# Column sums of squares on TensorE: a bfloat16 product of ones with the upper halves of the words in place of a float32 product

## The chip, the cores and the metric

The kernel runs on one core of one Trainium2 chip. The metric is the device time of one launch in microseconds (us), the median of several runs. Each of the core's engines works through a list of instructions of its own, in order: TensorE (PE: matrix products; its weight loads are shown apart, as PEld), VectorE (DVE), ScalarE (ACT), GpSimd (POOL) and SyncE (SP, which issues the DMAs here). They wait for each other on semaphores.

## The reference, cut to what matters

Two branches work on the same input x (2048 tokens, width 576) and a gate mixes them, token by token:

```python
g = sigmoid((x * gate_w).sum(-1, keepdims=True))
a = attention(x, wq, wk, wv, wo, beta)   # 32 heads of 18, 4 segments of 512 tokens, memory over segments
b = (gelu(x @ w_gate) * (x @ w_up)) @ w_down   # inner width 4608
return g * a + (1 - g) * b
```

Everything is float32. The kernel computes each product in pairs of float16 words: a number is scaled by a power of two, its float16 rounding is the upper word, the rest is the lower word, and a product takes three matrix products (high by high, high by low, low by high). The powers of two come from sums of squares of the operands, and this is all that these sums are for: a scale is read from the exponent of such a sum.

## The kernel before

**Stages.** The program first loads x and the attention weights and finds their scales (to about 25 us). Then the projections of the four segments run (to about 215 us). Then 72 steps follow, 36 tiles of the inner width by 2 halves of the tokens; `step(v)` interleaves the feed-forward products of a tile with the attention of the heads (lines 1263 `down`, 532 `product`, 1383 nested products, 1178 `scores`, 1216 `values`). Two tiles make a block of four steps, and a block takes 72.5 us. From about 1480 us the last down products and the output projection run (line 1739).

**Order of the work.** PE, ACT, DVE and POOL execute their instructions in the order in which the code issues them; nothing is moved by a planner. What makes an engine wait is data, a PSUM bank or a buffer that isn't free yet.

**A scale.** `sum_squares` (DVE) or `act_square` (ACT, line 89) squares a tile and leaves a sum for each partition in one column of a small tile: `wst` for the attention weights and the first x, `stat` for the feed-forward weights. The sum over the partitions is a matrix product with a 128x128 tile of ones: `sums` (line 94), with 10, 5 or 3 columns. DVE adds up the columns of the result (lines 108, 187 or 268) and makes the powers of two from the exponent.

**Where `sums` stands.** It is called 24 times:

- in the first 25 us four times, from `scale_x(0)`, `scale_sum(4)`, `scale_v` and `scale_sum(0)`, on `wst`;
- 19 times on `stat`, from `scales`: once in the projections of the last segment (159 us), once in the first step (215 us), then once in a block, in its second step, up to 1442 us;
- once from `scale_sum(2)`, in the last step (1472 us), on `wst`, for the output weights.

The tile of ones is float32 (`ones`), and so are `wst` and `stat`. Such a product stands as one instruction in the program's list and as two weight loads and two passes in the trace. A second tile of ones, `onesb`, is bfloat16; it is used for the 30 warm-up products at the start (line 819) and for the sums of squares of x (line 176).

Of the kernel before, what the change touches and what calls it, by code (L numbers as in the profile page):

```python
# [8 lines left out]
F32 = mybir.dt.float32  # L9
BF16 = mybir.dt.bfloat16  # L10
# [8 lines left out]
P = 128  # L19
# [24 lines left out]
def kernel(ctx: ExitStack, tc: tile.TileContext, xs, wqk, wv, wo, wgu, wd, beta, out):  # L44
    nc = tc.nc
    pe, act, dve, pool, sp = nc.tensor, nc.scalar, nc.vector, nc.gpsimd, nc.sync

    cst = ctx.enter_context(tc.tile_pool(name="cst", bufs=1))
# [4 lines left out]
    def bank(tag, bufs=1, dt=F32):  # L53
        return ps.tile([P, 512 if dt == F32 else 1024], dt, name=tag, tag=tag, bufs=bufs)
# [4 lines left out]
    def spare():  # L59

        turns["n"] += 1
        if not turns["of"]:
            return bank("st", 2)
        return bank("V") if turns["n"] % 3 == 0 and turns["of"] == 3 else bank("dn", 2)
# [26 lines left out]
    def sums(st, o=None):  # L91

        o = (spare() if o is None else o)[:, : st.shape[1]]
        pe.matmul(o, ones, st, start=True, stop=True)
        return o

    def scale_of(i, total):
# [8 lines left out]
    def scale_sum(i, st, o=None):  # L106
        t = wts.tile([P, 1], F32, name="sv", tag="sv", bufs=2)
        dve.tensor_reduce(t, sums(st, o), AX.X, OP.add)
        scale_of(i, t)
# [69 lines left out]
    def scale_x(c):  # L179
        one = slice(c, c + 1)  # L180
        n = x2[:, one]
        if c:
            norm_x(c, bank("pv") if c == 1 else spare())
            dve.tensor_scalar(n, n, x2[:, c - 1 : c] if c % 2 else 1e-30, None, OP.max)
        else:
            n = wts.tile([P, 1], F32, name="sv", tag="sv", bufs=2)
            dve.tensor_reduce(n, sums(wst[:, 5:10]), AX.X, OP.add)
            dve.tensor_scalar(n, n, 1e-30, None, OP.max)
        v = cst.tile([P, 2], F32, name="xv", tag="xv", bufs=2)
        root(v[:, 0:1], v[:, 1:2], n)  # L190

        dve.tensor_scalar(xsc[:, one], v[:, 1:2], 2.0**-52, None, OP.mult)
        dve.tensor_scalar(xis[:, one], v[:, 0:1], 2.0**51, None, OP.mult)
        x16[c] = wts.tile([P, 9, L], F16, name="x16", tag="x16", bufs=4)
# [69 lines left out]
    def scales(fb, o=None):  # L264

        o = sums(stat[fb % 2].rearrange("p a b -> p (a b)"), o)
        z = wts.tile([P, 6], F32, name="z", tag="z", bufs=2)
        dve.tensor_reduce(z[:, 4:6], o.rearrange("p (a b) -> p a b", a=2), AX.X, OP.add)
        dve.tensor_scalar(z[:, 0:4], x2, z[:, 4:5], 1e-30, OP.mult, OP.max)
        v = wts.tile([P, 2, 2], F32, name="v", tag="v", bufs=2)  # L270
        pb = wts.tile([P, 2, 4], F32, name="pb", tag="pb", bufs=3)
        dve.tensor_scalar(v[:, 0].bitcast(I32), z[:, 4:6].bitcast(I32), 1, EXP, OP.logical_shift_right, OP.bitwise_and)
        dve.tensor_scalar(pb[:, 0].bitcast(I32), z[:, 0:4].bitcast(I32), EXP, None, OP.bitwise_and)
        dve.tensor_scalar(v[:, 1].bitcast(I32), v[:, 0].bitcast(I32), EXP, None, OP.bitwise_xor)
        dve.tensor_scalar(pb[:, 1].bitcast(I32), pb[:, 0].bitcast(I32), EXP, None, OP.bitwise_xor)
        scl_a[fb] = v, pb
# [220 lines left out]
        oms.append(dram.tile([HT, D], F32, name="om"))  # L497
        oas.append(dram.tile([HT, 9 * P], F16, name="oa"))

    ones = cst.tile([P, P], F32, name="ones")  # L500
    onesb = cst.tile([P, P], BF16, name="onesb")
    mask = cst.tile([P, L], BF16, name="mask")
    gate = cst.tile([P, 3, 16], F32, name="gate")
# [51 lines left out]
    with tc.tile_pool(name="prj", bufs=2, side="right", reuse_waits="tile") as pp:  # L555
# [256 lines left out]
        FIRST = (0,)  # L812
        with tc.manual_schedule(engines=ORDERED):
            pool.memset(onesb, 1.0)
            pool.memset(ones, 1.0)

            start = bank("G")
            for _ in range(30):
# [293 lines left out]
    with tc.tile_pool(name="keep", bufs=2, side="right", reuse_waits="tile") as kp, ExitStack() as tail:  # L1112
# [679 lines left out]
        with tc.manual_schedule(engines=ORDERED):  # L1792
# [21 lines left out]
            for t in range(16):  # L1814
                for n in range(2):
                    down(fb, t, n)
                if t in (1, 2):
                    f, c, o, g = ends.pop(0)
# [80 lines left out]
```

## Time and profile before

| | us |
|---|---|
| median of 3 runs | 1559.5 |
| lowest and highest run | 1559.41, 1560.13 |
| span of the profiled execution, first to last instruction | 1558.8 |
| PE busy | 1552.4 |
| PE weight loads busy | 953.9 |
| DVE busy | 1264.4 |
| ACT busy | 1205.9 |
| POOL busy | 1133.1 |

The page gives no time for the profiled execution beside its span; the median of the runs stands 0.7 us above it. Busy times of matmuls overlap, since a matmul starts while the one before it still drains. What a matmul takes from PE's stream is therefore read from the distance between starts, not from its duration. [...]

### The profile page before, as it was taken

To read this page: it belongs to the slowest core of one execution; us is meant where nothing else is said; L and a number is where in the kernel's file an instruction comes from. 1 tells how busy PE (TensorE), PEld (TensorE's weight loads), DVE (VectorE), ACT (ScalarE), POOL (GpSimd) and SP (SyncE) were. 2 spreads that over 40 slices of the span, in tenths; PEclk is the share of its full clock that TensorE was granted. 3 is DMA by queue.
4 is the path that set the end of the run, shared out by engine and by line. 5 is a ranking of instruction groups with operands and counts; after the bars stand their busy time and mean duration, and the time that the engine had idled before them with its cause. 6 is when DMAs were issued, how large, how long until landed. Compare 5 with 4: busy or idle time off the path is not lost.

```text
span 1558.8 us, 33947 instructions
## 1 busy us (share of the span) xinstructions
PE 1552.4 (100%) x12220; PEld 953.9 (61%) x12220; DVE 1264.4 (81%) x3256; ACT 1205.9 (77%) x2059; POOL 1133.1 (73%) x1220
## 2 busy tenths in 40 slices
PE   9999999999999999999999999999999999999999
PEld 5765755565656666656656565666655666656577
DVE  7878986888888888888888888888888878887665
ACT  7667544888888888888788888888888888887421
POOL 4355566778787868686877878786868687787597
PEclk9999999999999999999999999999999999999999
DMA  6533332567868677777767786868687877764646
GB/s 233 214 126 120 138 116 70 115 126 124 148 123 151 119 157 133 130 138 134 141 126 135 124 151 123 149 122 164 135 130 134 140 137 134 136 113 99 125 91 166
DMA packets 472865, 209.97 MB, mean 135 GB/s; under 512 B 427720, under 2 KB 437448, under 8 KB 472184
## 3 DMA queue, kind: packets, MB, share of 16 engines
q1 hardware_dynamic: 472696, 207.80, 65.7%
q8 instruction: 96, 1.57, 0.4%
q14 instruction: 73, 0.60, 0.1%
HBM read 91.87 MB, written 27.26 MB: 76 GB/s over the span
## 4 chain that ended last, share of the span: by engine, by line
PE 87%; POOL 6%; DMA 2%; ACT 2%; DVE 1%; issue 1%; SPq 0%; POOLq 0%; ACTq 0%
PE dn L1263 24%; PE U L532 16%; PE G L532 11%; PE V L532 6%; PE V L1383 5%; PE pv L1216 4%; PE st L412 3%; PE dn L419 2%; PE U L1309 2%; PE U L412 1%; PE G L412 1%; PE V L1314 1%; PE st L1178 1%; PE G L1314 1%; POOL pairg L1715 1%; PE G L1309 1%
## 5 line engine op out<-in xcount | busy, mean ns | idle before, releaser
L1199 POOL TENSOR_TENSOR pb<-pb,ph 128x896 f16<-128x896 f32 (+1 forms) x256 | 368.8, 1441 | 243.9 <-ACT ph L1198 233.8
L532 PEld LDWEIGHTS <-pairg 128*128 128x128 f16 x2592 | 247.9, 98 | 257.2 <-issue 10.0
L1263 PE MATMUL dn<-paird,hhr 128*128 128x288 f16 x2115 | 328.8, 286 | 0.5 <-DVE acc L1271 0.5
L1197 ACT ACTIVATE pb<-pb,mb,esc 128x512 f32<-128x512 f32 (+3 forms) x512 | 305.0, 642 | 5.5 <-issue 0.4
L1271 DVE SCALAR_TENSOR_TENSOR acc<-dn,ev,acc 128x288 f32<-128x288 f32 x533 | 262.4, 513 | 38.3 <-PE dn L1263 32.8
L1263 PEld LDWEIGHTS <-hhr 128*128 128x128 f16 x2160 | 207.2, 98 | 78.6 <-issue 12.4
L532 PE MATMUL G<-x,pairg 128*128 128x512 f16 x864 | 209.9, 379 | 0.2 <-DVE gl L1286 0.2
L1263 PE MATMUL dn<-paird,hhd 128*128 128x288 f16 x1275 | 210.0, 286 | 0.1
L532 PE MATMUL U<-xt,pairg 128*128 128x512 f16 x864 | 209.9, 379 | 0.0
L1198 ACT ACTIVATE ph<-pb 128x896 f16<-128x896 f32 (+1 forms) x256 | 188.6, 737 | 8.1
L345 POOL TENSOR_TENSOR pairg<-raw,pairg 128x384 f16<-128x384 f32 (+2 forms) x144 | 157.8, 1117 | 16.8 <-ACT pairg L341 16.8
L1181 DVE CUSTOM_DVE_ANT_0 pb<-st,mask 128x512 f32<-128x512 f32 (+1 forms) x256 | 157.1, 613 | 1.4 <-DMA pt<-pb 1.2
L1263 PEld LDWEIGHTS <-hhd 128*128 128x128 f16 x1296 | 124.6, 98 | 50.4 <-issue 6.5
L1181 DVE CUSTOM_DVE_ANT_0 pb<-dn,mask 128x256 f32<-128x256 f32 (+1 forms) x192 | 67.1, 374 | 77.6 <-PE dn L1178 76.0
L1383 PE MATMUL V<-xt,nest 128*128 128x256 f16 x714 | 105.5, 272 | 0.0
L532 PE MATMUL U<-x,pairg 128*128 128x512 f16 x432 | 105.0, 379 | 0.0
L532 PE MATMUL V<-x,pairg 128*128 128x512 f16 x426 | 103.8, 379 | 0.1
L1304 ACT ACTIVATE gl<-gl,sc 128x512 f32<-128x512 f32 x110 | 75.8, 715 | 33.1 <-DVE gl L1573 21.3
L1216 PEld LDWEIGHTS <-pt 128*128 128x128 f16 x2560 | 80.8, 96 | 13.3 <-issue 8.4
L1301 POOL TENSOR_TENSOR hhr<-gl,hhr 128x512 f16<-128x512 f32 x64 | 78.6, 1234 | 10.9 <-ACT hhr L1293 10.8
L1216 PE MATMUL pv<-vt,pt 128*128 128x37 f16 x2560 | 85.2, 179 | 0.0
L341 ACT ACTIVATE pairg<-raw 128x384 f16<-128x384 f32 (+2 forms) x144 | 77.8, 588 | 8.5 <-DVE raw L307 6.1
(369 smaller groups left out, 3083.9 us busy)
## 6 DMA issues: line engine op xcount, KB each, us to landing
raw<-in_wgu_dram SPq DMA_DIRECT2D x36, 640.0 KB
rawd<-in_wd_dram SPq DMA_DIRECT2D x36, 288.0 KB
qt<-qk SPq DMA_DIRECT2D x132, 72.0 KB
kt<-qk SPq DMA_DIRECT2D x132, 72.0 KB
qk<-stage SPq DMA_DIRECT2D x36, 256.0 KB
qt<-qk SPq DMA_DIRECT2D x132, 36.0 KB
kt<-qk SPq DMA_DIRECT2D x132, 36.0 KB
vp<-vstage SPq DMA_DIRECT2D x16, 296.0 KB
```

What stands on the lines that cost most here:

```text
L345: pool.tensor_tensor(spot(f, *p, 1), raw_g[f][:, p[0] : p[1]], spot(f, *p, 0), OP.subtract)
L412: pe.matmul(o, w(k, a), x[:, i], start=n == 0, stop=n == 13, skip_group_check=True)
L532: pe.matmul(o, w[:, i, (a + k) * P : (a + k + 1) * P], x[:, b + k], start=start and k == 0 and i == 0 and b == h, stop=k == 1 and i == 1, ...
L1181: dve.tensor_tensor_reduce(scored(a, qi), out[qi], mask[:, L - (qi + 1) * P :], 1.0, -3e38, OP.add, OP.max, mx[a][:, qi : qi + 1])
L1197: act.activation(r, r, AF.Exp, bias=b[:, qi : qi + 1], scale=esc[:, 0, c : c + 1])
L1198: act.activation(h[:, cols], p, AF.Copy)
L1199: pool.tensor_tensor(low[:, cols], p, h[:, cols], OP.subtract)
L1216: pe.matmul(ov, pr[:, 10 * i + COL[qi] // P + kb], v[:, 4 * e + kb, c0 : c0 + VC], start=kb == 0 and i == 0, stop=kb == qi and i == 1)
L1263: pe.matmul(o[:, :NH], hh[:, a, q * P : (q + 1) * P], w[:, b, n * NH : (n + 1) * NH], start=i == 0, stop=i == 5)
L1271: dve.scalar_tensor_tensor(av, o[:, :NH], ev, av, OP.mult, OP.add)
L1301: pool.tensor_tensor(hh[:, 1], t, hh[:, 0], OP.subtract)
L1383: pe.matmul(o, w[:, (7 * c + i) * P : (7 * c + i + 1) * P], x[d], start=start and n == 0, stop=n == 2, skip_group_check=True)
```

## The change

`sums` multiplies with the bfloat16 tile of ones. Its other operand is the same tile of float32 words, seen as twice as many bfloat16 numbers, of which every second one, the upper half of each word, is taken. The upper half of a float32 word is the number cut to 8 bits of mantissa. The result in PSUM is float32 as before. The float32 tile of ones and its memset on POOL go.

```diff
     def sums(st, o=None):
         o = (spare() if o is None else o)[:, : st.shape[1]]
-        pe.matmul(o, ones, st, start=True, stop=True)
+        pe.matmul(o, onesb, st.bitcast(BF16)[:, 1::2], start=True, stop=True)
         return o
...
-    ones = cst.tile([P, P], F32, name="ones")
     onesb = cst.tile([P, P], BF16, name="onesb")
...
             pool.memset(onesb, 1.0)
-            pool.memset(ones, 1.0)
```

PE's list in a block, at the product on `stat`, before. `G` and `dn` are PSUM banks, `pv` is the bank that the sums go to, `x`, `pairg`, `hhd` and `paird` are operands of the feed-forward products; what follows "waits" names the engines whose semaphores are waited for:

```order
L1309 LDWEIGHTS pairg
L1309 MATMUL G<-x_1136,pairg 128x512
L94 MATMUL pv<-stat_88,ones 128x10 [waits DVE_49,PE_49,Activation_49]
L1263 LDWEIGHTS hhd_4384
L1263 MATMUL dn<-paird,hhd_4384 128x288
```

The same place of the changed kernel (two lines were removed, so later lines count two less):

```order
L1307 LDWEIGHTS pairg
L1307 MATMUL G<-x_1134,pairg 128x512
L94 LDWEIGHTS onesb [waits DVE_49,PE_49]
L94 MATMUL pv<-stat_87,onesb 128x10 [waits Activation_49]
L1261 LDWEIGHTS hhd_4382
L1261 MATMUL dn<-paird,hhd_4382 128x288
```

The neighbours are the same. The weight load stands on its own now, with the waits for the bank, and the wait for ACT, which writes the sums of squares, has gone to the matmul.

PE's list at the second of the four products of the start, `scale_sum(4)`, before; line 710 holds float32 products with v's raw weights (`acc`) and x (`raw`), line 412 the first projection, `wp` its weights:

```order
L710 MATMUL G<-acc,raw 128x290 [waits PE_49]
L94 MATMUL st<-wst,ones 128x5 [waits DVE_49,Activation_49]
L710 MATMUL G<-acc,raw 128x290 x3
L94 MATMUL pv<-wst,ones 128x5
L412 LDWEIGHTS wp [waits Activation_49]
```

And in the changed kernel:

```order
L709 MATMUL G<-acc,raw 128x290 [waits PE_49]
L94 LDWEIGHTS onesb [waits DVE_49]
L94 MATMUL st<-wst,onesb 128x5 [waits Activation_49]
L709 MATMUL G<-acc,raw 128x290 x3
L94 LDWEIGHTS onesb
L94 MATMUL pv<-wst,onesb 128x5
L412 LDWEIGHTS wp [waits Activation_49]
```

Here too the two waits are divided between the load and the matmul. All 24 products change in this way. The lists of DVE, ACT and SP are the same row by row; POOL's loses the one memset.

## Rows read from the trace of the kernel before

**Rows 1.** The page, part 4: share of the chain that ended last, by engine.

```profile
PE 87%; POOL 6%; DMA 2%; ACT 2%; DVE 1%; issue 1%; SPq 0%; POOLq 0%; ACTq 0%
```

**Rows 2.** Busy time by stretch: length, then each engine's busy us and instructions, clock, DMA.

```profile
215.00:1480.00 1265.00, 1264.26 (x10244) 759.44 (x10243) 1037.36 (x2750) 1051.94 (x1778) 962.41 (x1011) 1.00 0.70 130
```

**Rows 3.** Waits of PE: us in total, times, longest.

```profile
PE dn L1263 <- DVE acc L1271: 0.5, 2, 0.3
```

**Rows 4.** Instructions of line 94: ns min/median/max, first and last start in us.

```profile
L94 PE MATMUL pv<-stat,ones x32: 174/216/258, 282.4 to 1370.3; 128*128 128x10 f32 x32
...
L94 PE MATMUL dn<-stat,ones x6: 174/218/258, 159.4 to 1442.4; 128*128 128x10 f32 x6
...
L94 PE MATMUL st<-wst,ones x4: 245/249/253, 11.1 to 15.5; 128*128 128x5 f32 x4
...
L94 PE MATMUL pv<-wst,ones x4: 168/214/257, 17.2 to 24.6; 128*128 128x5 f32 x2, 128*128 128x10 f32 x2
```

**Rows 5.** PE's timeline, first and last of 19 products: start us, us, instructions.

```profile
159.38 0.29 PE L94 MATMUL dn<-stat,ones 128*128 128x10 f32 x2
159.52 0.65 PE L419 MATMUL dn<-wv,x 128*128 128x290 f16 x4
...
1442.18 0.38 PE L1309 MATMUL G<-x,pairg 128*128 128x512 f16 x1
1442.40 0.29 PE L94 MATMUL dn<-stat,ones 128*128 128x10 f32 x2
1442.54 0.65 PE L1263 MATMUL dn<-paird,hhd 128*128 128x288 f16 x4
```

**Rows 6.** PE's timeline at 20 short float16 products, and what follows them.

```profile
1365.49 0.67 PE L1216 MATMUL pv<-vt,pt 128*128 128x37 f16 x20
1366.01 0.38 PE L532 MATMUL V<-x,pairg 128*128 128x512 f16 x1
```

**Rows 7.** Timeline of all engines at one block's product.

```profile
426.25 0.19 ACT L89 ACTIVATION_READ_ACCUMULATOR nest<-rawd 128x1 f32 x1
...
426.49 0.33 PEld L94 LDWEIGHTS pv<-stat,ones 128*128 128x128 f32 x2 [0.19 <-ACT nest L89]
...
426.63 0.29 PE L94 MATMUL pv<-stat,ones 128*128 128x10 f32 x2
```

**Rows 8.** Timeline of all engines at the start's second product.

```profile
15.18 0.08 DVE L85 DVE_READ_ACCUMULATOR2_ANT wst<- 128x1 f32 x1
...
15.40 0.36 PE L94 MATMUL st<-wst,ones 128*128 128x5 f32 x2
...
15.80 0.16 DVE L108 TENSOR_REDUCE sv<-st 128x1 f32<-128x5 f32 x1 [0.54 <-PE st L94]
```

**Rows 9.** DVE's timeline behind it, then PE's at the first wait after it.

```profile
17.61 0.89 DVE L115 SCALAR_TENSOR_TENSOR wp<-acc,wsc,wp 128x640 f16<-128x640 f32 x1 [0.84 <-ACT wp L112]
18.42 2.18 DVE L216 SCALAR_TENSOR_TENSOR x<-raw,xsc,x 128x1024 f16<-128x1024 f32 x1
...
34.28 3.18 PE L412 MATMUL st<-x,wp 128*128 128x512 f16 x14 [0.39 <-DVE stage L670]
```

**Rows 10.** The chain that ended last, near the end, and PE's timeline at the last product.

```profile
1454.26 4.84 DMA orow<-oa
...
1463.89 2.27 POOL pairg L1715 x2
...
1471.86 0.28 PE L94 MATMUL dn<-wst,ones 128*128 128x3 f32 x2
```

**Rows 11.** Instructions on the float32 ones: the memset on POOL.

```profile
L815 POOL MEMSET ones<- x1: 206/206/206, 0.9 to 0.9; 128x128 f32 x1
```

**Rows 12.** Timelines of DVE and PE at a late transposing DMA.

```profile
1248.64 0.69 DVE L1181 CUSTOM_DVE_ANT_0 pb<-st,mask 128x512 f32<-128x512 f32 x1 [0.81 <-DMA pt<-pb]
...
1247.90 1.63 PE L1263 MATMUL dn<-paird,hhr 128*128 128x288 f16 x12
1249.82 0.90 PE L1263 MATMUL dn<-paird,hhr 128*128 128x288 f16 x6 [0.29 <-DVE acc L1271]
```

## The prediction

> **What bounds the kernel now.** I read four views, in this order. First the shares of the chain that ended last: PE holds 87% of it [rows 1]. Second the table by stretches, for the steps of the feed-forward part: PE is busy 1264.26 of 1265.00 us there, DVE, ACT and POOL 76 to 83% [rows 2], and the clock is at its higher level throughout, so what the change does to PE's stream isn't paid for in another clock. PE's waits confirm this: the one on DVE at the down products comes to 0.5 us [rows 3]. So in the middle of the program a nanosecond taken out of PE's stream should come off the end. Third, the instructions of line 94, to see what a sum takes now: each of the 24 products shows as two passes, so 32 and 6 passes on `stat` are 19 products, and 4, 4 and 2 passes on `wst` are five [rows 4, 10]. Fourth the timelines around them, since durations overlap and only the distance between starts tells what a product takes from the stream.
>
> **What a product costs now.** The first of the 19 on `stat` starts at 159.38 and the next product at 159.52; the last at 1442.40, the next at 1442.54 [rows 5]. That is 0.140 us in both, once before an f16 product of 290 columns and once before one of 288. In front of the last, a product of 512 columns starts at 1442.18, 0.22 us earlier, which is what 512 columns take anyway; the time is therefore not lost ahead of the sum but behind it. The piece of two passes lasts 0.29 us, and its longer pass 0.258 [rows 4], so the second pass starts about 0.03 us behind the first, and the following product 0.11 us behind the second. [...]
>
> **What it will cost.** The list shows one load and one pass of ten columns, from bfloat16 ones. Its nearest row is a product with its own 128x128 float16 load and 37 columns: 20 of these start at 1365.49 and what follows starts at 1366.01, so 0.026 us each, load included [rows 6]. I take this, since it is the same sequence with two-byte weights. The bounds: no cost at all (0.140 saved), and only the first pass saved (0.03 saved, 0.11 left, if the next load is as late behind a bfloat16 pass as behind a float32 one). A loss inside the product I exclude, because one load and one pass go and nothing is added to them.
>
> [...]
>
> So 0.140 - 0.026 = 0.114 us for each product whose saving reaches the end.
>
> **Which of the 24 count.** The 19 on `stat` stand between 159 and 1442 us, in the stretch in which PE's stream is the bound: 19 x 0.114 = 2.17 us. Bounds 19 x 0.03 = 0.57 and 19 x 0.140 = 2.66.
>
> The divided waits add nothing there. In a block the sum waits for ACT's last square. Its accumulator is read from 426.25, for 0.19 us, to 426.44; the load, which carries the wait now, goes at 426.49, and the first pass starts at 426.63, when the stream gets there [rows 7]. With the wait on the matmul the load can go before, and ACT is still 0.19 us early. Behind it on PE stand the down products; they would be late only if ACT fell behind by more than this.
>
> The second product of the start is on a chain of its own. DVE's last square ends at 15.26; the passes begin at 15.40 and last 0.36, to 15.76; DVE, which has waited 0.54 us, goes on at 15.80 [rows 8]. From there come the first scale, ACT's words, DVE's low words (it waits 0.84 us for ACT at 17.61 and then runs on without a gap), and PE's first projections; PE's own wait ends at 34.28, on DVE [rows 9]. One pass should last about 0.18 us, as one of the twenty does (0.67 - 19 x 0.026) [rows 6], so the chain gets 0.36 - 0.18 = 0.18 us. Bounds: nothing, if a DMA of the start binds somewhere in between, and 0.36.
>
> The other three of the start save their 0.1 us too, but PE waits afterwards for DVE and ACT, and these don't wait for them: nothing counted, 0.1 us each if the cover goes. The last product (1471.86) comes when the chain of the end has already left PE: it runs from a DMA at 1454.26 to POOL at 1463.89 [rows 10]. Nothing counted, 0.11 us if I misread it. The memset of 206 ns on POOL at 0.9 us [rows 11] goes while everything waits for the first loads: nothing counted, 0.2 us at most.
>
> **Sum.** 2.17 + 0.18 = 2.35 us. Against the profiled execution: a span of 1558.8 - 2.35 = 1556.45 us. The page shows no time of that execution beside the span, and the median of the runs stands 0.7 us above it; I keep this, which gives 1557.15, told as 1557.1 us, 0.15% less than 1559.5. A measurement of this kernel can tell about 0.2%, or 3.1 us, from no change. So the forecast is a gain that is real and too small to be told.
>
> **Rivals.**
>
> [...]
>
> *The gain is given back.* Each block gets 0.11 us shorter for PE, and some other engine needs its old period. For it: DVE, at 1037 of 1265 us, and ACT, at 1052, aren't far off. Against it: these follow PE's progress step by step, and PE's waits on DVE are only 0.5 us now [rows 3]. Price: 1559.3, only the start's share remaining.
>
> *Late transposing DMAs (the slower side).* The attention words go through a DMA transpose, and DVE may write the next scores only when the buffer is free. At 1248.64 DVE has waited 0.81 us for such a DMA, and PE, which started twelve products of 288 columns at 1247.90 (0.12 us each at the higher clock) and should have gone on at about 1249.37, does so at 1249.82: some 0.45 us lost [rows 12]. DMA engines are 70% busy [rows 2] with as many bytes as before, in shorter blocks. From six more such waits on the gain is gone, and from 13 on the kernel is slower by more than 3.1 us; at 13 it would be 1557.1 + 5.9 = 1563.0. Against it: PE's waits on DVE at the down products are two in the whole trace [rows 3], and a block changes by 0.11 of 72.5 us.
>
> *More than that.* The product costs nothing, the start gains 0.36, and the 0.5 us of waits on DVE [rows 3], the last product's 0.11 and the memset's 0.2 go as well: 2.66 + 0.36 + 0.5 + 0.11 + 0.2 = 3.83, so 1555.7 us.
>
> That the change doesn't do what it says, I exclude: the list shows it in all 24 places.
>
> **Chances.** Forecast (1556.4 to 1558.0): 0.62. Next load not hidden: 0.10. Given back: 0.12. Late DMAs: 0.07. More than that: 0.09. The range goes from 1555.7, the lower end of all bounds, to 1559.3, the price of a gain given back. It leaves out the late DMAs and part of the two last cases. Faster by over 0.2% means below 1556.4: most of the last case and a tenth from the forecast, if the start or the irregular waits give more, 0.17. Slower by over 0.2%: 0.07. The rest, 0.76, lies within.
>
> **What the profile after would show.** Line 94 with 24 passes and 24 loads in place of 48 and 48, so 12196 matmuls; the following product 0.025 to 0.03 us behind the pass, not 0.14; blocks 0.11 us shorter from product to product; DVE's reduction at the start about 0.2 us earlier behind its last square, and PE's wait of 34.28 earlier by as much; the end's DMA and POOL chain unchanged in length and moved as a whole. I am wrong if the distance behind the pass stays at 0.1 us, if PE's wait for ACT appears at line 94, or if the blocks keep their 72.5 us although the distance has shrunk.

## The result, and the profile after

The changed kernel takes 1565.31 us (median of 6 runs, 1564.32 to 1566.65), the kernel before 1560.01 us in the same comparison: ratio 1.0035, 95% interval 1.0024 to 1.0046. It is 5.3 us slower. I had forecast 1557.1 us, in a range up to 1559.3.

**The product itself did what was forecast.** The page's head and first row, then the instructions of line 94:

```profile
span 1564.7 us, 33892 instructions
...
PE 1551.8 (99%) x12196; PEld 950.3 (61%) x12196; DVE 1266.1 (81%) x3256; ACT 1206.0 (77%) x2059; POOL 1130.5 (72%) x1219
```

```profile
L94 PEld LDWEIGHTS <-onesb x24: 95/98/98, 11.5 to 1477.9; 128*128 128x128 bf16 x24
...
L94 PE MATMUL pv<-stat,onesb x16: 170/170/170, 283.2 to 1376.7; 128*128 128x10 bf16 x16
...
L94 PE MATMUL dn<-stat,onesb x3: 170/170/170, 160.1 to 1448.7; 128*128 128x10 bf16 x3
```

PE makes 12196 matmuls in all. Each of the 24 sums has one load and one pass, where [rows 4] shows two passes; the rows here are the 24 loads and the 19 passes on `stat`. PE's timeline at one block's sum, the same as in [rows 7]:

```profile
427.19 0.38 PE L1307 MATMUL G<-x,pairg 128*128 128x512 f16 x1
427.40 0.17 PE L94 MATMUL pv<-stat,onesb 128*128 128x10 bf16 x1
427.43 0.40 PE L1261 MATMUL dn<-paird,hhd 128*128 128x288 f16 x2
```

The following product starts 0.03 us behind the sum (0.028 in the trace's nanoseconds) and not 0.14 as in [rows 5]. All 21 products that stand in a running stream (the 19, the fourth of the start and the last) save 0.11 us. The granted clock is 1.00 over the whole profile after; in the one before it is 1.00 in [rows 2] and 0.50 in the last 0.8 us (1558.0 to 1558.8), when no engine is busy any more.

**The time went to a wait that was hardly there before.** Waits of all engines, then PE's alone: us in total, times, longest. Line numbers are one or two lower than before (1179 is 1181, 1381 is 1383):

```profile
DVE pb L1179 <- DMA pt<-pb: 10.3, 9, 2.4
```

```profile
PE V L1381 <- DVE hold L1397: 5.7, 7, 1.9
```

DVE waits nine times for a transposing DMA before it may overwrite a buffer of attention words. In the kernel before there were two such waits, one of them at [rows 12]:

```profile
DVE pb L1181 <- DMA pt<-pb: 1.2, 2, 0.8
```

Seven times PE then waits for DVE, at a nested product in a block's fourth step; the kernel before had no wait of PE at this line. One of them, in the timelines of SP (the DMA's issue), DVE and PE:

```profile
479.86 3.39 SPq L1200 DMA_TRANSPOSE pt<-pb  x1
...
487.56 0.69 DVE L1179 CUSTOM_DVE_ANT_0 pb<-st,mask 128x512 f32<-128x512 f32 x1 [1.06 <-DMA pt<-pb]
488.17 0.08 DVE L1179 DVE_READ_ACCUMULATOR2_ANT mx<- 128x1 f32 x1
488.17 0.42 DVE L1397 COPY hold<-V 128x256 f32<-128x256 f32 x1
...
487.60 0.53 PE L1261 MATMUL dn<-paird,hhd 128*128 128x288 f16 x3
488.64 0.49 PE L1381 MATMUL V<-xt,nest 128*128 128x256 f16 x3 [0.51 <-DVE hold L1397]
```

DVE stands 1.06 us in front of the scores, the copy that frees a bank for PE stands behind them, and PE goes on 0.68 us late (three products of 0.12 us started at 487.60).

By stages, from the trace's times: to the first block's sum 282.36 us before and 283.25 after; from there to the last block's sum 1087.96 and 1093.49; from there to the end 188.48 and 187.92. So the loss lies in the 15 blocks between. Counted from start to start, the time that PE spends in front of the nested products of line 1381 grew by 6.7 us.

**Why the DMA is late.** A transposing DMA reports its landing in 16 parts (the page counts 16 DMA engines). The records of this one, and of the same DMA before (us):

```
after   485.121 485.127 485.130 ... (15 parts up to 485.227), then 487.532
before  485.562 485.569 485.573 ... (16 parts up to 485.717)
```

Fifteen parts land together and one lags by 2.3 us. What lies in between is on the page, in part 3, and in the DMA view of 484.5 to 485.8 us: queue, kind, packets, MB, share.

```profile
q8 instruction: 96, 1.57, 0.4%
q14 instruction: 73, 0.60, 0.1%
```

```profile
q8 instruction: 1, 0.02, 5.0%
```

Queue q8 makes 96 fetches of 16 KB over the span. PE's list in the trace is 24565 instructions, 256 for each fetch, so I take it that this queue feeds PE; experiments 9 and 10 bear that out. By these numbers, 16 KB and 256, an instruction takes 64 bytes. PE itself loses next to nothing to the fetches: 80 of them fall into the stretch of [rows 2], in which PE isn't busy for 0.74 us in all. One fetch starts at 484.66, 0.5 us before the fifteen parts land. All nine waits of DVE have a fetch that starts 2 to 4 us before they end, in this sequence within a block (us behind the block's sum):

```
              a fetch at                DVE's wait ends at    (blocks counted from 0)
after         36.4 to 37.7              40.1 to 40.7          blocks 1, 5, 9, 13
after         57.3 to 58.0              60.1 to 61.5          blocks 2, 6, 10, 14
after         19.8                      23.4                  block 12
before        19.9                      23.8                  block 13
before        34.8, 34.4, 32.8, 33.2    no wait               blocks 1, 5, 9, 13
before        56.8, 51.4, 51.7, 50.8    no wait               blocks 2, 6, 10, 14
```

The kernel before's other wait (0.43 us, block 12) has no fetch near it.

The fetch makes a transpose late in two ways. In five of the nine waits (blocks 2, 6, 10, 12 and 14) one part of the awaited DMA lags, by 1.6 to 3.0 us. In the other four (blocks 1, 5, 9 and 13) its 16 parts land within 0.3 us of each other, but at 40.0 to 40.7 us instead of 39.1: there the fetch starts while the transpose issued just ahead is under way, that one lands 1.2 to 1.9 us late, and the awaited one about 1 us behind it.

How often a fetch at this place does it can be counted over all 14 traces, the experiments' among them. Of 3808 transposing DMAs 68 have a last part more than 1 us behind the fifteenth. For 65 of the 68 a fetch on q8 started 0.44 to 0.77 us before the fifteenth part landed. Of the 109 transposes with a fetch at that place 65 have such a lag, of the 3699 others 3. One of the 3 has a fetch on q14, the other instruction queue, 0.66 us ahead of it. Fetches on q14 are of 8 KB and leave smaller lags: over 0.5 us in 66 of the 116 transposes that have one 0.4 to 0.8 us ahead (and none on q8), against 10 of the 3577 with neither. Which engines q14 feeds the trace doesn't say.

A block of the kernel before has 1217 instructions of PE, 4.75 fetches, so the places repeat after about four blocks. The change takes a load and a pass out at every sum; with the waits that have a row of their own, PE's list is 24619 long in the trace before and 24565 after. So from sum to sum the fetches come later in the block, and reach places where a transposing DMA has no time to lose.

### The profile page after: what moved, and what is told of

The parts are those of the page before. It is cut to its first block, busy times and chain, and to the rows that moved or that the text cites. A ratio compares the mean times of both kernels' runs of the same rounds, so it can differ in the third digit from the quotient of the medians.

```text
span 1564.7 us, 33892 instructions
## 1 busy us (share of the span) xinstructions
PE 1551.8 (99%) x12196; PEld 950.3 (61%) x12196; DVE 1266.1 (81%) x3256; ACT 1206.0 (77%) x2059; POOL 1130.5 (72%) x1219
## 5 line engine op out<-in xcount | busy, mean ns | idle before, releaser
L1190 ACT ACTIVATE mb<-mx,esc 128x4 f32<-128x4 f32 x128 | 36.4, 284 | 65.8 <-DVE mx L1179 65.8
L1381 PEld LDWEIGHTS <-nest 128*128 128x128 f16 x714 | 67.2, 97 | 31.4 <-issue 7.3
```

What stands on the lines that cost most here:

```text
L1381: pe.matmul(o, w[:, (7 * c + i) * P : (7 * c + i + 1) * P], x[d], start=start and n == 0, stop=n == 2, skip_group_check=True)
```

## The experiments

Theory A says that this place decides. Theory B: the blocks, 0.11 us shorter, outrun the transposes wherever the fetches fall. All times are medians; each run was compared with the kernel before on the same chip.

**1. The changed kernel, 30 instructions more at the start.**

```diff
-            for _ in range(30):
+            for _ in range(45):
                 pe.matmul(start[:, :P], onesb, onesb, start=True, stop=True)
```

> The changed kernel with 45 warm-up products in place of 30: 30 instructions more ahead of everything on TensorE, done before the first loads land, nothing else changed. Theory A (TensorE's instruction list has become shorter, so that its 16 KB instruction fetches fall later in a block, and those that start just before a transposing DMA of the attention words lands hold back one sixteenth of it): fetches move about 1.8 us earlier in each block, away from the places 36 to 38 and 57 to 58 us behind a block's sum, so DVE's waits for the transposes fall from 10.3 us to under 3 and the time to 1557 to 1560 us. Theory B (each block has become 0.11 us shorter on TensorE and the transposes no longer keep up, wherever the fetches fall): unchanged, 1564 to 1567 us, waits 8 us or more.

1560.24 us, ratio to before 0.9998 (0.9989 to 1.0008). The waits for transposes:

```profile
DVE pb L1179 <- DMA pt<-pb: 2.6, 4, 1.0
```

This is at the upper end of what A expects (0.24 us over it), and B falls. 5 us come back for 15 warm-up products. The fetches now start at 32.9 to 34.8 us in blocks 1, 5, 9 and 13, where the changed kernel had 36.4 to 37.7. Two of the four waits left (blocks 5 and 13, 0.6 and 1.0 us) have no fetch on q8 2 to 4 us before their end, but one on q14 2.0 to 2.5 us before it; that q14's fetches cause them was not tried.

But the forecast gain isn't there: blocks without a late DMA take 72.45 to 72.54 us. (Left out here and below is the first block, 71.7 us, and block 11, which is long in the kernel before too, 72.99 us, as PE waits for DVE and POOL there.)

**2. The kernel before, 30 instructions fewer** (15 warm-up products in place of 30).

> The kernel before with 15 warm-up products in place of 30: 30 instructions fewer ahead of everything on TensorE. Theory A (place of the instruction fetches): fetches move about 1.8 us later in each block, those at 34.4 and 34.8 us behind a block's sum come to the place 36 to 37, so DVE waits for late transposes come to 3 us or more and the time to 1561 to 1565 us, without any of the change. Theory B (shorter blocks): 1559.5 to 1560.5 us, waits 1 to 2 us as before.

1566.31 us, ratio 1.0040 (1.0028 to 1.0053), a little over the upper end expected. Without any of the change the kernel before becomes as slow as the changed one:

```profile
DVE pb L1181 <- DMA pt<-pb: 9.6, 11, 2.5
```

Its fetches stand at 37.6, 37.7 and 37.7 us in blocks 1, 5 and 9 and at 58.3 in block 2, with waits behind each. Three of the eleven waits (blocks 0, 8 and 13) have no fetch on q8 at that distance; all three have one on q14 1.2 to 2.6 us before their end.

**3. The sum's bfloat16 product made twice.**

```diff
-        pe.matmul(o, onesb, st.bitcast(BF16)[:, 1::2], start=True, stop=True)
+        for _ in range(2):
+            pe.matmul(o, onesb, st.bitcast(BF16)[:, 1::2], start=True, stop=True)
```

> The changed kernel with each sum's bfloat16 product made twice into the same bank (two loads and two passes, as many instructions as the float32 product before has in the trace). Theory A (place of the instruction fetches): the fetches fall as in the kernel before, waits for transposes under 3 us, and the time is that of before less 19 x (0.140 - 0.056): 1557.5 to 1560 us. Theory B (shorter blocks): the blocks are still 0.08 us shorter than before, so 1563 to 1567 us.

1559.82 us, ratio 0.9995 (0.9985 to 1.0004), as A expects; DVE's waits for transposes shrink to

```profile
DVE pb L1180 <- DMA pt<-pb: 0.4, 1, 0.4
```

The list has its old length but for 6 instructions (24613 and 24619), and the waits are all but gone. Again the blocks stay at 72.50 to 72.53 us, but for the one with the late transpose (72.94), though each sum is 0.08 us cheaper than before.

**4. The changed kernel, 54 instructions more at the start** (57 warm-up products).

> The changed kernel with 57 warm-up products in place of 30: 54 instructions more, which is what its list is shorter by at the end of the program. Theory A (place of the instruction fetches): fetches move about 3 us earlier in a block, to the places of the kernel before in the second half of the program, waits under 3 us, 1557 to 1560 us. Theory B (shorter blocks): 1564 to 1567 us.

1567.96 us, ratio 1.0045 (1.0030 to 1.0060). My expectation failed: in the middle of the program the changed list is not yet 54 instructions shorter, so 54 more put the fetches elsewhere than in the kernel before. A itself holds, since DVE's waits come to

```profile
DVE pb L1179 <- DMA pt<-pb: 8.9, 4, 3.3
```

with fetches at 37.6 us in block 2 and at 57.4, 58.2 and 59.1 in blocks 3, 7 and 11, and those four blocks are the long ones (72.7, 74.1, 75.1 and 77.2 us).

**Where the 0.11 us of a block go when no DMA is late.** I laid PE's products of a block before and of experiment 1 side by side. They run 0.112 us early from the sum on, and 27.75 us further, at a product into bank G, 0.10 of it is gone. DVE, POOL and PE there, before and then with 45 warm-up products:

```profile
380.01 1.11 DVE L1246 SCALAR_TENSOR_TENSOR ob<-ob,wsc,oh 128x576 f16<-128x576 f32 x1
381.04 0.74 DVE L1286 SCALAR_TENSOR_TENSOR gl<-G,sc,gl 128x512 f32<-128x512 f32 x1
...
379.78 0.73 POOL L333 TENSOR_TENSOR raw<-raw 128x256 f32<-128x256 f32 x1
...
380.57 1.47 PE L532 MATMUL V<-x,pairg 128*128 128x512 f16 x6
381.87 1.46 PE L532 MATMUL G<-x,pairg 128*128 128x512 f16 x6
```

```profile
379.36 1.25 DVE L1244 SCALAR_TENSOR_TENSOR ob<-ob,wsc,oh 128x576 f16<-128x576 f32 x1
380.53 0.74 DVE L1284 SCALAR_TENSOR_TENSOR gl<-G,sc,gl 128x512 f32<-128x512 f32 x1
...
379.27 0.73 POOL L333 TENSOR_TENSOR raw<-raw 128x256 f32<-128x256 f32 x1
...
379.91 1.47 PE L531 MATMUL V<-x,pairg 128*128 128x512 f16 x6
381.32 1.46 PE L531 MATMUL G<-x,pairg 128*128 128x512 f16 x6
```

DVE frees G at 381.78 before and PE takes it at 381.87: PE has next to no room there. With the shorter sum the six products into V take 1.41 us to the next start, not 1.30. DVE is still at `result_low` (the first DVE row), which took 1.25 us in place of 1.11.

Why it takes longer can be read from POOL's row. In both kernels `result_low` ends 0.61 us behind the end of POOL's operation (380.51 and 381.12; 380.00 and 380.61). That operation keeps its distance behind the block's sum (25.65 and 25.69 us), while `result_low` starts 0.11 us earlier, with PE: it starts sooner and ends at the same place. Over all 14 traces 117 of the 210 `result_low` in these blocks started while an operation of POOL still had 0.3 us or more to run; each took more than 0.83 us and ended 0.61 to 0.62 us behind that operation. Where DVE starts 0.05 us ahead of POOL, as in block 11 of the kernel before, it takes 0.81 us and POOL's operation 1.35 in place of 0.73:

```profile
1105.24 0.81 DVE L1246 SCALAR_TENSOR_TENSOR ob<-ob,wsc,oh 128x576 f16<-128x576 f32 x1
...
1105.29 1.35 POOL L333 TENSOR_TENSOR raw<-raw 128x256 f32<-128x256 f32 x1
```

In block 11 of experiment 1 `result_low` takes 0.81 us too, and PE's six products keep their 1.31 us. So one of the two engines is held up by the other although no data passes between these operations; data, banks and buffers are not all that an engine waits for here. No run moved POOL's operation, so its part is read from traces alone.

Theory C: this wait gives the gain back. Theory D: another engine holds the block at 72.5 us wherever `result_low` stands. Experiments 5 to 8, 11 and 12 move `result_low` behind the next step's first down products, where DVE waits 1 us for PE:

```diff
-            low = (k - 6) // 4 if k % 4 == 2 and 0 <= (k - 6) // 4 < H // 2 - 1 else None
+            low = (k - 7) // 4 if k % 4 == 3 and 0 <= (k - 7) // 4 < H // 2 - 1 else None
...
             puts.pop(2 * k - 1, None)
+            if low is not None:
+                result_low(low)
...
-            if low is not None:
-                result_low(low)
             if fb:
                 low_rests(f, (X, U4, x1), (Y, UG, x2_))
```

**5. With two passes.**

> The kernel with each sum's bfloat16 product made twice, and DVE's low words of the attention result (result_low, 1.1 to 1.25 us on DVE, once a block) issued in the next step, behind that step's first down products, where DVE waits 1 us for TensorE, instead of ahead of the product that frees bank G. Theory C (the 0.08 to 0.11 us that a block gains at the sum are given back 27.75 us further on, where TensorE waits for bank G, because DVE is still at result_low): the undisturbed blocks go from 72.51 to 72.42 us, that wait is gone, and the time is 1.0 to 1.6 us below that of the kernel with two passes (1559.8): 1558.2 to 1559. Theory D (some other engine holds the block at 72.5 us): blocks stay at 72.5 us and the time at 1559.5 to 1560.5 us.

1557.82 us, ratio 0.9985 (0.9976 to 0.9994), a little better than expected. All blocks but the first, block 11 included, take 72.41 to 72.43 us, as C expects. DVE now frees G early, and the product into G follows V's without a wait:

```profile
380.58 0.75 DVE L1285 SCALAR_TENSOR_TENSOR gl<-G,sc,gl 128x512 f32<-128x512 f32 x1 [0.36 <-PE G L1313]
...
380.68 1.47 PE L532 MATMUL V<-x,pairg 128*128 128x512 f16 x6
381.99 1.24 PE L532 MATMUL G<-x,pairg 128*128 128x512 f16 x5
```

**6. With one pass and 45 warm-up products.**

> The changed kernel with 45 warm-up products and result_low moved in the same way: one pass for each sum. Theory C: undisturbed blocks of 72.40 us and 1.5 to 2 us less than with 45 warm-up products alone (1560.2): 1558 to 1559 us. Theory D: blocks 72.5 us, 1560 to 1560.7 us.

1557.50 us, ratio 0.9979 (0.9969 to 0.9988): a little better than expected. Blocks take 72.39 us, but for two with a late transpose (72.67 and 73.07). This beats both kernels.

**7. The control: the kernel before with `result_low` moved.**

> The kernel before with result_low moved in the same way, nothing else. TensorE's wait for bank G is about nothing there, so theory C expects no gain: blocks 72.50 us and 1559.8 to 1561 us, unless the move shifts other waits. Theory D: the same. It is the control: what the move gives without the change to the sums.

1560.45 us, ratio 0.9999 (0.9990 to 1.0008), blocks 72.50 to 72.52 us, but for two with a late transpose (73.03 and 73.33). The move alone gives nothing; it lets the sum's gain through.

**8. As 6, with 40 warm-up products.**

> As with 45 warm-up products and result_low moved, but with 40: 10 instructions fewer, the instruction fetches some 0.6 us later in a block. Theory A (place of the fetches) expects the same undisturbed blocks (72.40 us) and another set of late transposes: between 1558 and 1563 us, and whatever stands above 1558.5 is found in DVE's waits for transposes. If a time above that comes without such waits, theory A isn't the whole of it.

1558.27 us, ratio 0.9987 (0.9978 to 0.9997). One block is long (73.65 us), and DVE's waits come to 2.4 us.

**Is it the place, or the length of the list?** One fetch is 256 instructions. Two kernels make the list longer, by warm-up products of 10 columns behind the others:

```diff
+            for _ in range(128):
+                pe.matmul(start[:, :10], onesb, onesb[:, :10], start=True, stop=True)
```

**9. The changed kernel and 256 instructions more.**

> The changed kernel with 128 more warm-up products of 10 columns behind the 30: 256 instructions more, some 3.5 us of TensorE's time before the first loads land. 256 instructions of 64 bytes are one fetch of 16 KB, so theory A (place of the instruction fetches) expects every fetch at the place of the changed kernel again: DVE's waits for transposes near 10 us and 1564 to 1568 us, although 30 more instructions brought it to 1560.2. A rival A' (a longer list, or a longer warm-up, is what helps) expects 1557 to 1561 us.

1569.52 us, ratio 1.0055 (1.0038 to 1.0072), 1.5 us over the upper end. The waits are those of the changed kernel:

```profile
DVE pb L1181 <- DMA pt<-pb: 12.3, 9, 3.4
```

Nine again, in the same nine blocks, behind fetches at 36.7 to 37.7, 57.4 to 58.4 and 20.1 us. 30 instructions more mend it, 256 more don't. Of the 4.2 us above the changed kernel, the start has most: the first block's sum comes at 286.5 us and not 283.25, so the longer warm-up wasn't free.

**10. The kernel before and 226 more** (113 products), 30 short of a fetch.

> The kernel before with 113 more warm-up products of 10 columns: 226 instructions more, which is 30 fewer than one fetch of 256. Theory A expects the fetches where they are with 15 warm-up products (30 fewer): waits for transposes of 8 us or more and 1564 to 1568 us. Rival A' (fewer instructions or a shorter warm-up is what costs) expects 1559.5 to 1561 us, since the list is longer here.

1568.32 us, ratio 1.0056 (1.0041 to 1.0071), a little over; here the first sum comes 3 us late too.

```profile
DVE pb L1183 <- DMA pt<-pb: 9.1, 9, 2.5
```

Seven of the nine waits have a fetch on q8 2 to 4 us before their end. A list 226 longer is as bad as the one of experiment 2, 30 shorter. The rival A' falls.

**11. The changed kernel with `result_low` moved**, 30 warm-up products.

> The changed kernel with result_low moved into the next step, 30 warm-up products as in the change. If the two causes add (late transposes by the place of the fetches, and the gain given back at bank G), only the second is mended here: DVE's waits for transposes stay at 6 us or more, undisturbed blocks take 72.39 us, and the time is 1561 to 1565 us.

1562.78 us, ratio 1.0019 (1.0009 to 1.0028), with a wide spread (1559.88 to 1567.79). Nine late transposes remain (7.7 us of DVE's waits), in the blocks without them 72.39 us. Both causes are there, and moving `result_low` mends its own part alone.

**12. As 6, with 43 warm-up products.**

> As with 45 warm-up products and result_low moved, with 43: 4 instructions fewer, fetches 0.2 us later in a block. Looking for a place of the fetches with fewer late transposes (2.3 us of DVE's waits at 45, 2.4 at 40): 1556.5 to 1558.5 us, undisturbed blocks 72.39 us.

1558.11 us, ratio 0.9988 (0.9979 to 0.9998); 2.4 us of waits. No better than 45.

## Why the prediction was wrong

- **The cost of a product** was right: 0.028 us for 0.026 forecast, 0.112 saved for 0.114. The next load starts 1 to 2 ns behind the pass of ten columns and lasts 97 to 98 ns, yet its product starts 28 to 29 ns behind the pass: the case that the load isn't hidden, to which I had given 0.10, falls. In the kernel before, the second float32 load of each of these 21 sums starts 1 to 2 ns behind the first pass and lasts 190 to 192 ns, the load behind it lasts 181 ns, and the following product starts 0.140 to 0.142 us behind the first pass. That the second load is what costs the 0.11 us is my reading of these records; no run shows it by itself.
- **The start's second product** was right in kind: DVE's reduction comes 0.36 us behind its last square (16.31 and 15.95) where it was 0.62 [rows 8], so 0.26 for 0.18. It didn't show in the result, since that square itself came 0.77 us later. The first block's sum stood between 281.92 and 283.26 us over the profiled executions of experiments 1 to 8; what sets this I leave open.

```profile
15.95 0.08 DVE L85 DVE_READ_ACCUMULATOR2_ANT wst<- 128x1 f32 x1
...
16.09 0.18 PE L94 MATMUL st<-wst,onesb 128*128 128x5 bf16 x1 [0.24 <-DVE wst L85]
16.31 0.16 DVE L108 TENSOR_REDUCE sv<-st 128x1 f32<-128x5 f32 x1 [0.27 <-PE st L94]
```

- **"In the middle of the program a nanosecond taken out of PE's stream should come off the end"** is the step that failed, in both directions. PE's busy share and the 0.5 us of waits showed that PE waits for nobody, not that the others have room. At bank G DVE was 0.09 us ahead of PE, and 0.10 of a block's 0.11 us went there. The rival "given back" was right about the undisturbed blocks, and so was the sign that I had named, blocks that keep their 72.5 us although the distance has shrunk. My ground against it, that DVE and ACT follow PE's progress step by step, left out POOL, which does not follow here and holds DVE's `result_low`. Experiments 5 to 7 show that the gain is lost at this place.
- **The late transposing DMAs**, to which I gave 0.07, decide the result. DVE's wait at the scores I had right; the price was too low (0.45 us a wait for PE, measured 0.8, 5.7 us in 7 waits), and PE's loss stands at the nested products, not at the down products. I held it unlikely because a block changes by 0.11 of 72.5 us, and saw no way from the change to that DMA. The way is PE's own instruction list: I had counted the change's instructions only as work. The program's list shows 24 rows more, the trace 54 instructions fewer, since a float32 product is one row and four instructions; that shift, under 5% of a block's 1217 instructions at its largest, put fetches onto transposes in nine blocks. Experiments 1 to 3, 9 and 10 show it.
- **The sum** would have been near the mark with both removed: experiment 6 gains 2.9 us, 0.21% (0.12 to 0.31), where 2.35 us were forecast, with two late transposes left in it.

## What to carry to other kernels

That an engine is never idle says what bounds the kernel, not how much of a gain will pass: look along the next period for the waits that end just in time, and read how much room each has. Here an edit that took 54 of 24619 instructions off PE's list moved its instruction fetches against the transposes, with 5.3 us more in the result, and 30 instructions more at the start gave 5.1 us back (1565.31 and 1560.24). So a change of a few tenths of a per cent should be timed at two or three lengths of the list (15 warm-up products at the start were enough here) before it is believed, either way.

## What the runs showed of the hardware that I had not expected

- An instruction fetch of 16 KB takes mostly 0.9 to 1.6 us on its queue. A transposing DMA whose other parts landed 0.44 to 0.77 us behind the start of such a fetch had one of its 16 parts 1.4 to 3.4 us late in 65 of 109 cases. Why the lag is longer than the fetch was not tried; nor was a buffer more for the attention words, which should take the wait away.
- With the same work, 15 warm-up products more or fewer at the start move the time by 5 to 6 us: 1560.7 to 1566.3 before, 1565.3 to 1560.2 after. The 15 more put PE's first product at 5.34 us in place of 4.26, which is gone by the first block's sum (281.92 and 283.25 us).
- The same operation on DVE (128x576, float32 to float16) took 0.81 us, or up to 1.26 where an operation of POOL still had 0.3 us or more to run at its start; it then ended 0.61 to 0.62 us behind that one.
